# Attention and a gated layer on one core: raw scores of batches 1 to 7 stored with even and odd rows side by side, and the product of W3 and W_out started earlier and by halves of W_out

## The chip, the core and the metric

The kernel runs on one core of a Trainium2 chip. The metric is the device time of one execution in microseconds. Before the change, three runs took 1436.35 to 1438.15 us, with a median of 1437.4 us. The profiled execution took 1441.87 us, and its span from the first to the last instruction is 1439.9 us.

## What is computed

The reference is attention with two head mixings, followed by a layer of four matrices, all in float32. B = 8 batches, H = 12 heads, S = 448 rows and columns of scores, D = 64.

```python
scores = scale * np.matmul(q, k.transpose(0, 1, 3, 2))
scores = np.einsum('bhij,hg->bgij', scores, w_pre)
scores = scores - np.max(scores, axis=-1, keepdims=True)
attn = np.exp(scores)
attn = attn / (np.sum(attn, axis=-1, keepdims=True) + 1e-09)
attn = np.einsum('bhij,hg->bgij', attn, w_post)
x = np.matmul(attn, v)          # then (B, S, H, D) -> (B * S, 768)
...
a = x @ w1
b = x @ w2
h = a * b @ w3
return h @ w_out
```

## The kernel before

**Raw scores.** The product of queries and keys is made per batch b, head pair p and quarter c of the rows (`qk`, L167). One unit (b, p, c) is four matmuls into two PSUM banks, `psq`; ScalarE copies both banks into an SBUF tile `st` (L180, L181), and a store puts `st` into a scratch tensor in device memory, `raw_d[b]`, of the shape (row, head, column). The quarters c = 0, 1, 2 have 128 rows, and c = 3 holds the last 64 rows of two head pairs, so a batch has 18 + 3 = 21 units. `st` has two buffers in each of two pools: one pool serves batches 1 to 7 and the even p of batch 0, the other the odd p of batch 0. Through `raw_d` the scores change their layout, since the mixing of heads needs (row, head) on the partitions.

**Blocks.** The rows of a batch are cut into NB = 45 blocks of IB = 10 rows, the last of 8. Two blocks form one m. `fetch` (L196) loads both blocks of m into a tile `r` (two buffers), as two halves s of five rows by twelve heads, 60 partitions each; `mix` (L215) multiplies by w_pre into the banks `psm`; `largest` (VectorE, L228) and `exp` (ScalarE, L236) follow; `scale` (L240) makes the weights w_post divided by the sums on GpSimd; `post` (L251) multiplies by them into the banks `pso`, and `put` (L273) copies these on ScalarE into `mt` (L275). After every GB = 15 blocks, `av` (L293) multiplies `mt` by V (`psa`, L302).

**The order of the work.** `run` (L744) writes out one program over N = 360 steps n, one per block. An even step n = 2m has `largest` and `exp` of m, an odd one `scale` of m, `post` of m - 1 and `mix` of m + 1. So the distance between the exp of two following m is the length of two steps, and the stages of the trace are cut there: in the profiled execution exp of step 10 starts at 59.31 us, of step 18 at 98.42 us. Within a step the order is: fetch (even steps), stores and loads that are due (`do_later`), one piece of weight conversion, `largest` or `scale`, part of the background matmuls (`advance`), `exp`, the rest of these, `av`, `post`, `mix`, and at last the units `qks[n]`. A unit's store is issued at the start of the next step. All DMAs are issued by SyncE in program order; each waits for the completion of the DMA eight places before it, as they share eight semaphores.

**Which unit in which step.** Batch 0 has c = 0 ahead of the loop, then one unit per step in steps 0 to 14. Batch 1's 21 units start at step 11 with 28/21 steps between two of them (L817), so steps 11 to 13 have two units each. The keys and queries of a pair (`kq`) are loaded six steps ahead of its first unit.

**Fold.** The weights come as float64, read as pairs of int32. `converting` (L133) turns one piece of 384 or 256 columns per step into float32 with four VectorE instructions (L122 to L125) and a square on ScalarE (L111), none in steps with `av`; in the step after, `two_parts` (L128) splits it into a high part (ScalarE, L130) and a low part (GpSimd, L131). From W3 and W_out their product is made, called the fold: 8 columns f of W3 (`fw[f]`, three pieces each) by two halves of W_out (`fo`, eight pieces each), each group (f, half) being 8 x 3 = 24 matmuls of 128x384 (`psf`, L361) into bank 6 or 7, 384 in all. The pieces come in the order: column 0, both halves of W_out, then columns 1 to 7 (L330). `there(p)` (L869) says how many fold matmuls the pieces made so far allow; `share` (L851) spreads the fold over steps FOLD = 18 to 48, as it evens out their TensorE work. The first 24 are made by step 9 as the pieces come.

After step 50 the background is the layer itself (`eg`, `eo`, `e`, L523 to L704); a tail of it follows the last step.

Of the kernel before, what the change touches and what calls it, by code (L numbers as in the profile page):

```python
# [18 lines left out]
IB = 10  # L19
# [31 lines left out]
class Kernel:  # L51
# [115 lines left out]
    def qk(self, b, p, c, banks):  # L167


        nc = self.nc  # L170
        ps = [self.bank(i, f"psq{b}_{p}_{c}_{s}")[:, :S] for s, i in enumerate(banks)]
        for z, (t, q, k) in enumerate(self.parts(b, p, c)):
            for s in range(2):
                rows = slice(s * D, (s + 1) * D)
                nc.tensor.matmul(ps[s][z * PP:(z + 1) * PP], t[rows, q:q + PP], t[rows, k:k + S], start=True, stop=True)  # L175
# [4 lines left out]
        nc.scalar.copy(st[:, 0], ps[0])  # L180
        (nc.vector.tensor_copy if b == c == 0 else nc.scalar.copy)(st[:, 1], ps[1])  # L181
        raw = self.raw_d[b]
        if c == 3:
            def store():
                for z in range(2):
                    nc.sync.dma_start(raw[3 * QT:, 2 * (p + z) - 2:2 * (p + z)], st[z * PP:(z + 1) * PP])
            return store
        n = QT if b or c else FIRST
        return lambda: nc.sync.dma_start(raw[c * QT:c * QT + n, 2 * p:2 * p + 2], st[:n])
# [6 lines left out]
    def fetch(self, m):  # L196
        r = self.rp.tile([128, 2, S], F32, tag="r", name=f"r{m}", bufs=2)
        self.rs[m] = r
        b, t = divmod(2 * m, NB)
        if t + 1 < NB and self.width(2 * m + 1) == IB:  # L200
            src = self.raw_d[b][t * IB:(t + 2) * IB].rearrange("(c s i) h j -> s (i h) c j", c=2, s=2)
            for s in range(2):
                self.nc.sync.dma_start(r[s * PP:s * PP + HK], src[s])
            return
        for c in range(2):
            b, t = divmod(2 * m + c, NB)
            for s in range(2):
                k = self.half(2 * m + c, s)
                src = self.raw_d[b][t * IB + s * IH:t * IB + s * IH + k].rearrange("i h j -> (i h) j")
                self.nc.sync.dma_start(r[s * PP:s * PP + H * k, c], src)  # L210

    def half(self, n, s):
        return min(IH, self.width(n) - s * IH)

# [36 lines left out]
    def post(self, m):  # L251
# [11 lines left out]
        for c in range(2):  # L263
            n = 2 * m + c
            w, (b, t) = self.width(n), divmod(n, NB)
            a, u = divmod(t, GB)
            if u == 0:
                self.mt[b, a] = self.mp.tile([128, NJ, H, GB * IB], F32, tag="mt", name=f"mt{b}_{a}")
            src = self.pso[c][:, :NJ * 2 * HK].rearrange("p (j s g i) -> p j s g i", j=NJ, s=2, g=H)
            dst = self.mt[b, a][:, :, :, u * IB:u * IB + w]  # L270
            self.ends.append((4 + c, lambda dst=dst, src=src, w=w: self.put(dst, src, w)))

    def put(self, dst, src, w):  # L273
        if w == IB:
            self.nc.scalar.copy(dst.rearrange("p j g (s i) -> p j s g i", s=2), src)  # L275
# [54 lines left out]
    def fold_jobs(self):  # L330
# [17 lines left out]

    def folding(self):
        nc = self.nc  # L350
        for f in range(KF):
            for half in range(2):
                w = self.fw[f]

                i = 6 + half
                p = self.bank(i, f"psf{half}_{f}")[:, :DH]
                atoms = [(k, t, x, y) for k in range(KF) for t, (x, y) in enumerate(PAIRS)]
                for k, t, x, y in atoms:
                    if (k, t) != (0, 0):
                        yield  # L360
                    nc.tensor.matmul(p, w[:, k, x], self.fo[:, k, y, half * DH:(half + 1) * DH],  # L361
                                     start=(k == 0 and t == 0), stop=(k == KF - 1 and t == 2))
                z = self.fp.tile([128, 3, 2, 128], F32R, tag="z", name=f"fz{half}_{f}")
                q = p.rearrange("p (d c) -> p d c", c=128)
                dst = self.w34_d[half * 3:(half + 1) * 3, :, f].rearrange("d p t c -> p d (t c)")

                def low(z=z, q=q, dst=dst):
                    nc.vector.tensor_tensor(z[:, :, 1], q, z[:, :, 0].bitcast(F32), op=ALU.subtract)
                    self.later.append(lambda: nc.sync.dma_start(dst, z.rearrange("p d t c -> p d (t c)").bitcast(F32)))

                self.ends.append((i, lambda z=z, q=q: nc.scalar.copy(z[:, :, 0], q)))
                self.soon.append((i, low))
                yield

# [369 lines left out]
    def run(self):  # L744
# [8 lines left out]
        self.ps = self.pool("ps", 1, space=PSUM)  # L753
        self.raw_d = [dp.tile([S, H, S], F32, name=f"raw{b}_d") for b in range(B)]
        self.w_d = [dp.tile([KF, 128, k, 2, 128], F32, name=f"w{i}_d") for i, k in enumerate((K1, K1, KF))]
# [137 lines left out]
        for n in range(N + 6):  # L893
# [48 lines left out]
            elif fold_pieces:  # L942
                f = (self.n_made - 1 - 2 * KF) // 3
                if f < 2 or done >= 2 * KF * 3 * (f - 1):
                    pieces = fold_pieces
# [72 lines left out]
def layouts(inputs):  # L1018
# [37 lines left out]
```

## Time and profile before

| | |
|---|---|
| runs, median (3) | 1437.4 us |
| profiled execution | 1441.87 us, span 1439.9 us |
| TensorE busy | 1386.1 us (96%) |
| VectorE, ScalarE, GpSimd busy | 742.8, 833.3, 622.0 us |
| mean granted TensorE clock | 0.987 |
| DMA | 416.87 MB, queue of SyncE 87.5% of 16 engines' span |

How to read it: a TensorE that is busy nearly all the time bounds the kernel wherever it has no gaps, so the places of interest are the gaps, and what ends them. In a row of the windows view stand the length of the stretch, each engine's busy time with the count of its instructions in brackets, the granted TensorE clock, the mean busy share of the 16 DMA engines and the rate in GB/s. A row of the timeline has start, length, engine, line, operation and operands, and in square brackets the engine's idle time ahead of it with what ended it.

### The profile page before, as it was taken

The numbers are of one execution on the slowest core, as the hardware profiler recorded it, in microseconds if no ns is written. First come the engines' busy times: TensorE is split into PE (matmuls) and PEld (weight loads), VectorE is DVE, ScalarE is ACT, GpSimd is POOL, SyncE is SP. The second block draws the span as 40 slices with busy tenths as digits, with TensorE's granted clock in tenths as the row PEclk, the third lists the DMA queues.
The fourth block names the chain that finished last, engine by engine and source line by source line (L and its number), as shares of the span: only waits on it lengthen the run. The fifth ranks groups of instructions, "written<-read, shape, count | busy, mean of one in ns | idle before, by whom it ended". The sixth has DMA issues, their size and how long they took to land.

```text
span 1439.9 us, 45779 instructions
## 1 busy us (share of the span) xinstructions
PE 1386.1 (96%) x18684; PEld 1056.7 (73%) x18684; DVE 742.8 (52%) x1497; ACT 833.3 (58%) x1952; POOL 622.0 (43%) x754
## 2 busy tenths in 40 slices
PE   5879999999999999999999999999999999999998
PEld 2357786766677767776777777777777777889988
DVE  5957566767644545432344435334444456345563
ACT  4866666767756756665655556556556445432231
POOL 1423233444324544532345345434335436457693
PEclk8989999999999999999999999999999999999999
DMA  8998789999999999999889988799979757698775
GB/s 283 366 319 277 237 266 321 325 312 305 313 280 356 368 357 318 380 348 333 286 266 290 315 289 265 247 316 332 300 229 301 248 174 224 196 327 268 239 234 171
DMA packets 203761, 416.87 MB, mean 290 GB/s; under 512 B 20528, under 2 KB 120112, under 8 KB 203472
## 3 DMA queue, kind: packets, MB, share of 16 engines
q1 hardware_dynamic: 203552, 413.94, 87.5%
q8 instruction: 149, 2.44, 0.7%
q14 instruction: 60, 0.49, 0.1%
HBM read 279.77 MB, written 134.09 MB: 287 GB/s over the span
## 4 chain that ended last, share of the span: by engine, by line
PE 81%; DMA 9%; DVE 5%; ACT 2%; issue 1%; SPq 0%; POOL 0%; DVEq 0%; POOLq 0%; ACTq 0%
PE e L704 20%; PE psa L302 11%; PE pso L261 10%; PE psm L221 8%; PE psq L175 7%; PE eg L523 6%; PE psf L361 4%; PE eo L554 4%; PE e2o L704 4%; PE e3o L704 4%; DMA wu<-w_d 3%; PE e1o L704 3%; DMA raw_d<-st 2%; DMA cs<-wo 2%; DMA r<-raw_d 1%
## 5 line engine op out<-in xcount | busy, mean ns | idle before, releaser
L248 POOL TENSOR_SCALAR w<-wpo,ri 128x60 f32<-128x60 f32 x360 | 180.3, 517 | 482.9 <-DVE ri L246 464.6
L228 DVE TENSOR_REDUCE mn<-psm 128x1 f32<-128x448 f32 x360 | 207.6, 618 | 319.1 <-PE psm L221 318.8
L275 ACT COPY mt<-pso 128x480 f32<-128x480 f32 x352 | 197.8, 621 | 183.6 <-PE pso L261 183.4
L704 PE MATMUL e<-eh,wu 128*128 128x448 f32 x1008 | 297.3, 371 | 4.4 <-DVE c L658 3.2
L236 ACT ACTIVATE e<-psm,mn 128x448 f32<-128x448 f32 x360 | 226.8, 643 | 8.3 <-DVE mn L228 8.3
L704 PEld LDWEIGHTS e<-eh,wu 128*128 128x128 f32 x1008 | 187.5, 188 | 50.9 <-issue 25.1
L221 PE MATMUL psm<-r,wsc 60*64 60x448 f32 (+1 forms) x1440 | 193.1, 552 | 20.7 <-DVE cx L124 7.8
L261 PEld LDWEIGHTS pso<-w,e 60*64 60x64 f32 x10080 | 175.3, 135 | 50.9 <-issue 42.2
L261 PE MATMUL pso<-w,e 60*64 60x60 f32 x10080 | 199.2, 224 | 0.4 <-ACT mt L275 0.3
L704 PE MATMUL e<-el,wu 128*128 128x448 f32 x504 | 186.8, 371 | 0.0
L302 PE MATMUL psa<-mt,v 128*64 128x150 f32 (+1 forms) x2304 | 158.5, 294 | 4.2 <-ACT st L180 4.2
L302 PEld LDWEIGHTS psa<-mt,v 128*64 128x64 f32 x2304 | 145.1, 138 | 20.3 <-ACT st L180 6.9
L175 PE MATMUL psq<-kq 64*64 64x448 f32 x1176 | 156.1, 542 | 4.0 <-ACT st L180 4.0
L658 DVE TENSOR_TENSOR c<-c,e 128x448 f32<-128x448 f32 x168 | 101.6, 617 | 82.5 <-PE e L704 77.9
L180 ACT COPY st<-psq 128x448 f32<-128x448 f32 x162 | 86.5, 534 | 79.7 <-ACT mt L275 34.1
L523 PE MATMUL eg<-xh,wu 128*128 128x448 f32 x384 | 118.8, 380 | 3.3 <-DMA wu<-w_d 3.3
L643 POOL TENSOR_TENSOR el<-x,eh 128x448 fp32r<-128x448 f32 x90 | 104.2, 1174 | 34.4 <-ACT eh L642 28.9
L704 PEld LDWEIGHTS e<-el,wu 128*128 128x128 f32 x504 | 94.6, 188 | 22.2 <-issue 14.1
L175 PEld LDWEIGHTS psq<-kq 64*64 64x64 f32 x1176 | 60.7, 135 | 58.1 <-issue 30.0
L523 PEld LDWEIGHTS eg<-xh,wu 128*128 128x128 f32 x384 | 71.4, 189 | 36.0 <-issue 24.7
L245 DVE TENSOR_SCALAR sa<-sm 128x2 f32<-128x2 f32 x180 | 35.2, 196 | 116.0 <-ACT e L236 115.6
L181 ACT COPY st<-psq 128x448 f32<-128x448 f32 x162 | 87.8, 542 | 0.0
(99 smaller groups left out, 2015.6 us busy)
## 6 DMA issues: line engine op xcount, KB each, us to landing
r<-raw_d SPq DMA_DIRECT2D x344, 210.0 KB, 5.4
raw_d<-st SPq DMA_DIRECT2D x138, 448.0 KB, 6.2
wu<-w_d SPq DMA_DIRECT2D x104, 384.0 KB, 6.4
wu<-s_d SPq DMA_DIRECT2D x96, 384.0 KB, 4.9
wu<-w_d SPq DMA_DIRECT2D x51, 512.0 KB, 6.2
kq<-kq SPq DMA_DIRECT2D x42, 448.0 KB, 7.1
wu<-s_d SPq DMA_DIRECT2D x36, 512.0 KB, 5.0
x<-x_d SPq DMA_DIRECT2D x72, 224.0 KB, 6.4
```

The costliest lines, as they stand in the source:

```text
L175: nc.tensor.matmul(ps[s][z * PP:(z + 1) * PP], t[rows, q:q + PP], t[rows, k:k + S], start=True, stop=True)
L221: nc.tensor.matmul(ps[s][c * PP:(c + 1) * PP, :S], self.wsc[k], r[k, c], start=True, stop=True)
L228: self.nc.vector.tensor_reduce(mn[:, s:s + 1], self.psm[m][s][:, :S], axis=AX.X, op=ALU.min)
L236: nc.scalar.activation(e, p[:, :S], AF.Exp, bias=mn[:, s:s + 1], scale=-1.0, accum_out=sm[:, s:s + 1])
L248: nc.gpsimd.tensor_scalar_mul(w2[:, s], self.wpo, ri[:, s:s + 1])
L261: nc.tensor.matmul(self.pso[c][z * PP:(z + 1) * PP, at:at + HK], e[k, j * PP:(j + 1) * PP], w2s[k, s], start=True, stop=True)
L275: self.nc.scalar.copy(dst.rearrange("p j g (s i) -> p j s g i", s=2), src)
L302: nc.tensor.matmul(self.psa[rows, g % 3, :W], v[:, j, rows], mt[:, j, 2 * g + s, :W], start=(j == 0), stop=(j == NJ - 1))
L523: nc.tensor.matmul(p, u[:, k % (K1 // 2), x], xs[y][:, k], start=(k == 0 and t == 0), stop=(k == K1 - 1 and t == 2))
L643: nc.gpsimd.tensor_tensor(lo, x, hi.bitcast(F32), op=ALU.subtract)
L658: nc.vector.tensor_tensor(a[out], a[to[0]], p, op=ALU.add)
L704: nc.tensor.matmul(p, w[:, k, x], ops[m, k][y], start=(k == 0 and t == 0), stop=(k == nk - 1 and t == 2))
```

## The change

Three things change.

**Raw scores of batches 1 to 7 are interleaved.** `raw_d[b]` has the shape (row pair, head, parity, column) for b > 0. The host orders the query columns so that in each unit the even rows lie on one half of the partitions and the odd ones on the other. A unit's store becomes two DMAs, one per parity (four for c = 3), whose contiguous runs in device memory are one head's 448 columns (1792 bytes) where they were two heads' (3584 bytes). A fetch of two blocks reads ten row pairs: the first block of m gets the even rows and the second the odd ones, and each partition reads one run of 3584 bytes where it read two of 1792. Blocks whose partner lies in another batch or in another group of 15, or is shorter, are fetched singly, with four DMAs. `put` writes `mt` with a stride of two elements for b > 0. Batch 0 stays as it was.

**Fold.** The pieces come as column 0, the first half of W_out, column 1, the second half of W_out, columns 2 to 7. The groups are (0, first half), (1, first half), then columns 0 and 1 with the second half together, k by k, then the others one after another. FOLD is 9.

**Batch 1's units** start at step 15, with 1.15 steps between two of them, so that no step before 48 has more than one unit.

By the rules of the loop, the matmuls of the fold that are done by the end of a step are:

| step | 9 | 11 | 13 | 15 | 17 | 18 | 21 | 24 | 25 | 31 | 41 | 48 |
|---|---|---|---|---|---|---|---|---|---|---|---|---|
| before | 24 | 24 | 24 | 24 | 24 | 43 | 58 | 99 | 106 | 180 | 288 | 384 |
| after | 24 | 42 | 54 | 66 | 78 | 84 | 96 | 114 | 144 | 220 | 305 | 384 |

Of batch 1's units, 6 come by the end of step 17 before, and 3 after.

TensorE, steps 11 and 12, before: the names are psq, batch, pair, quarter, bank. The rows run from the end of step 11 to the end of step 12.

```order
L175 MATMUL psq0_5_2_0_845<-kqz5_134 64x448
L175 MATMUL psq0_5_2_1_846<-kqz5_134 64x448
...
L175 MATMUL psq1_0_0_0_854<-kq1_0_468 64x448
L175 MATMUL psq1_0_0_1_855<-kq1_0_468 64x448
...
L175 MATMUL psq0_1_3_0_887<-kqz0_124 64x448
L175 MATMUL psq0_1_3_1_888<-kqz0_124 64x448
...
L175 MATMUL psq1_0_1_0_896<-kq1_0_468 64x448
L175 MATMUL psq1_0_1_1_897<-kq1_0_468 64x448
```

The same place after; psf is followed by half and column.

```order
L175 MATMUL psq0_5_2_0_863<-kqz5_134 64x448
L175 MATMUL psq0_5_2_1_864<-kqz5_134 64x448
...
L383 MATMUL psf0_1_772<-fo_148,fw1_691 128x384 x6
L175 MATMUL psq0_1_3_0_905<-kqz0_124 64x448
L175 MATMUL psq0_1_3_1_906<-kqz0_124 64x448
...
L383 MATMUL psf1_0_935<-fo_148,fw0_227 128x384 x3
L383 MATMUL psf1_1_936<-fo_148,fw1_691 128x384 x3
```

Two units of batch 1 have gone from between those of batch 0, and twelve fold matmuls of two columns stand between them.

TensorE, steps 22 to 24, before: the folds of steps 22 and 23, the mix of step 23, its unit, and the fold of step 24.

```order
L361 MATMUL psf0_1_1334<-fo_148,fw1_1127 128x384 x14
L361 MATMUL psf1_1_1481<-fo_148,fw1_1127 128x384 x12
...
L221 MATMUL psm12_0_1544<-r12_1309,wsc_138 64x448
L221 MATMUL psm12_1_1545<-r12_1309,wsc_138 64x448
...
L175 MATMUL psq1_2_2_0_1552<-kq1_2_986 64x448
L175 MATMUL psq1_2_2_1_1553<-kq1_2_986 64x448
...
L361 MATMUL psf1_1_1481<-fo_148,fw1_1127 128x384 x12
L361 MATMUL psf0_2_1598<-fo_148,fw2_1451 128x384 x3
```

The same place after, from the fold of step 23 to that of step 25.

```order
L383 MATMUL psf0_2_1519<-fo_148,fw2_1486 128x384 x9
...
L240 MATMUL psm12_0_1557<-r12_1344,wsc_138 64x448
L240 MATMUL psm12_1_1558<-r12_1344,wsc_138 64x448
...
L383 MATMUL psf0_2_1519<-fo_148,fw2_1486 128x384 x9
L175 MATMUL psq1_2_1_0_1607<-kq1_2_1144 64x448
L175 MATMUL psq1_2_1_1_1608<-kq1_2_1144 64x448
...
L383 MATMUL psf0_2_1519<-fo_148,fw2_1486 128x384 x6
L383 MATMUL psf1_2_1646<-fo_148,fw2_1486 128x384 x24
```

In steps 22 and 23 nine fold matmuls are left of 26, since the pieces allow no more, and step 25 has 30 at once.

SyncE, stores of units of batch 1's pair 1, before and after (each row with the number of like DMAs):

```order
L189 DMA raw1_d_63<-st1_1_0_1078 128x896
L104 DMA cs23_1089<-w3t 128x3x256
L189 DMA raw1_d_63<-st1_1_1_1114 128x896
L104 DMA cs24_1118<-w3t 128x2x256
L203 DMA r11_1183<-raw0_d_62 60x2x448 x2
```

```order
L189 DMA raw1_d_63<-st1_1_1_1341 64x2x448 x2
L158 DMA kq1_3_1349<-kq 128x896
L104 DMA cs26_1351<-w3t 128x3x256
L189 DMA raw1_d_63<-st1_1_2_1376 64x2x448 x2
L216 DMA r13_1472<-raw0_d_62 60x2x448 x2
```

A unit's one store has become two of half the size at the same place of the queue.

The diff, cut to its core:

```diff
         raw = self.raw_d[b]
+        if b:
+            n, parts = (PP // 2, ((2 * p - 2, 0), (2 * p, PP))) if c == 3 else (PP, ((2 * p, 0),))
+
+            def store():
+                for h, k in parts:
+                    for z in range(2):
+                        nc.sync.dma_start(raw[c * PP:c * PP + n, h:h + 2, z], st[k + z * n:k + (z + 1) * n])
+            return store
...
+        if self.paired(2 * m):
+            src = self.raw_d[b][t * IH:(t + 2) * IH].rearrange("(s i) h c j -> s (i h) c j", s=2)
+            for s in range(2):
+                self.nc.sync.dma_start(r[s * PP:s * PP + HK], src[s])
+            return
...
+    def paired(self, n):
+
+        t, u = n % NB, (n ^ 1) % NB
+        return n >= NB and n // NB == (n ^ 1) // NB and t // GB == u // GB and self.width(n) == self.width(n ^ 1) == IB
...
+            elif self.paired(n):
+                dst = self.mt[b, a][:, :, :, (u - c) * IB:(u - c + 2) * IB].rearrange("p j g (s i c) -> p c j s g i", s=2, c=2)[:, c]
...
-        yield from columns[0]
         for q in range(2):
+            yield from columns[q]
...
-        for f in range(1, KF):
+        for f in range(2, KF):
...
+        for group in [((0, 0),), ((1, 0),), ((0, 1), (1, 1))] + [((f, half),) for f in range(2, KF) for half in range(2)]:
...
+            for k in range(KF):
+                for f, half in group:
+                    for t, (x, y) in enumerate(PAIRS):
+                        self.nc.tensor.matmul(ps[f, half], self.fw[f][:, k, x], self.fo[:, k, y, half * DH:(half + 1) * DH],
...
-            first, per = (11, 28 / 21) if b == 1 else ((b - 1) * NB - 6, NB / 21)
+            first, per = (15, 1.15) if b == 1 else ((b - 1) * NB - 6, NB / 21)
...
-        FOLD, SWITCH, E_AT = 18, NB + 5, NB + 8
+        FOLD, SWITCH, E_AT = 9, NB + 5, NB + 8
...
-            f, r = divmod(p - 3 - 2 * KF, 3)
-            return 2 * KF * 3 * (1 + f) + (0, 9, 18)[r] if f >= 0 else min(max(3 * (p - 3), 0), KF * 3)
+            f, r = divmod(p - 6 - 2 * KF, 3)
+            if f >= 0:
+                return 2 * KF * 3 * (2 + f) + (0, 9, 18)[r]
+            if p >= 6 + KF:
+                return 2 * KF * 3 + 6 * (p - 6 - KF)
+            return KF * 3 + (0, 9, 18)[p - 3 - KF] if p >= 3 + KF else 3 * max(p - 3, 0)
...
-    kq = np.ascontiguousarray(np.stack([qt.reshape(B, HP, 2 * D, S), kt], axis=3))
+    order = [c + 2 * i + z for c, n in ((0, QT), (QT, QT), (2 * QT, QT), (3 * QT, PP)) for z in range(2) for i in range(n // 2)]
+    kq = np.ascontiguousarray(np.stack([qt.reshape(B, HP, 2 * D, S)[..., order], kt], axis=3))
```

More of the change, by code (lines that the diff above doesn't have):

```diff
@@ L187, in qk @@
             return store
-        n = QT if b or c else FIRST
+        n = QT if c else FIRST
         return lambda: nc.sync.dma_start(raw[c * QT:c * QT + n, 2 * p:2 * p + 2], st[:n])
@@ L199, in fetch @@
         b, t = divmod(2 * m, NB)
-        if t + 1 < NB and self.width(2 * m + 1) == IB:
+        if self.paired(2 * m):
[3 more added lines that the diff above has]
+            return
+        if b == 0 and t + 1 < NB and self.width(2 * m + 1) == IB:
             src = self.raw_d[b][t * IB:(t + 2) * IB].rearrange("(c s i) h j -> s (i h) c j", c=2, s=2)
@@ L208, in fetch @@
                 k = self.half(2 * m + c, s)
-                src = self.raw_d[b][t * IB + s * IH:t * IB + s * IH + k].rearrange("i h j -> (i h) j")
+                raw = self.raw_d[b][t * IH:t * IH + k, :, s] if b else self.raw_d[b][t * IB + s * IH:t * IB + s * IH + k]
+                src = raw.rearrange("i h j -> (i h) j")
                 self.nc.sync.dma_start(r[s * PP:s * PP + H * k, c], src)
     def half(self, n, s):
-        return min(IH, self.width(n) - s * IH)
+        return min(IH, self.width(n) - s * IH) if n < NB else self.width(n) // 2
+    def paired(self, n):
+        t, u = n % NB, (n ^ 1) % NB
+        return n >= NB and n // NB == (n ^ 1) // NB and t // GB == u // GB and self.width(n) == self.width(n ^ 1) == IB
     def mix(self, m):
@@ L269, in post, with put @@
             src = self.pso[c][:, :NJ * 2 * HK].rearrange("p (j s g i) -> p j s g i", j=NJ, s=2, g=H)
[L270 to L274, printed above, removed]
+            if b == 0:
+                dst = self.mt[b, a][:, :, :, u * IB:u * IB + w]
+            elif self.paired(n):
+                dst = self.mt[b, a][:, :, :, (u - c) * IB:(u - c + 2) * IB].rearrange("p j g (s i c) -> p c j s g i", s=2, c=2)[:, c]
+            else:
+                src = src[:, :, :, :, :w // 2]
+                dst = self.mt[b, a][:, :, :, u * IB:u * IB + w].rearrange("p j g (i s) -> p j s g i", s=2)
+            self.ends.append((4 + c, lambda dst=dst, src=src, w=w, b=b: self.put(dst, src, w, b)))
+    def put(self, dst, src, w, b):
+        if b:
+            self.nc.scalar.copy(dst, src)
+        elif w == IB:
             self.nc.scalar.copy(dst.rearrange("p j g (s i) -> p j s g i", s=2), src)
@@ L349, in folding @@
     def folding(self):
-        nc = self.nc
[L351 to L373, printed above, removed]
@@ new lines, in folding @@
+        for group in [((0, 0),), ((1, 0),), ((0, 1), (1, 1))] + [((f, half),) for f in range(2, KF) for half in range(2)]:
+            banks = {g: 6 + (g[0] if g[0] < 2 else g[1]) for g in group}
+            ps = {g: self.bank(banks[g], f"psf{g[1]}_{g[0]}")[:, :DH] for g in group}
+            for k in range(KF):
+                for f, half in group:
+                    for t, (x, y) in enumerate(PAIRS):
+                        self.nc.tensor.matmul(ps[f, half], self.fw[f][:, k, x], self.fo[:, k, y, half * DH:(half + 1) * DH],
+                                              start=(k == 0 and t == 0), stop=(k == KF - 1 and t == 2))
+                        if (k, t) == (KF - 1, 2):
+                            self.fold_out(f, half, banks[f, half], ps[f, half])
+                        yield
@@ new lines, in fold_out, with low @@
+    def fold_out(self, f, half, i, p):
+        nc = self.nc
+        z = self.fp.tile([128, 3, 2, 128], F32R, tag="z", name=f"fz{half}_{f}")
+        q = p.rearrange("p (d c) -> p d c", c=128)
+        dst = self.w34_d[half * 3:(half + 1) * 3, :, f].rearrange("d p t c -> p d (t c)")
+        def low():
+            nc.vector.tensor_tensor(z[:, :, 1], q, z[:, :, 0].bitcast(F32), op=ALU.subtract)
+            self.later.append(lambda: nc.sync.dma_start(dst, z.rearrange("p d t c -> p d (t c)").bitcast(F32)))
+        self.ends.append((i, lambda: nc.scalar.copy(z[:, :, 0], q)))
+        self.soon.append((i, low))
@@ L753, in run @@
         self.ps = self.pool("ps", 1, space=PSUM)
-        self.raw_d = [dp.tile([S, H, S], F32, name=f"raw{b}_d") for b in range(B)]
+        self.raw_d = [dp.tile([S // 2, H, 2, S] if b else [S, H, S], F32, name=f"raw{b}_d") for b in range(B)]
         self.w_d = [dp.tile([KF, 128, k, 2, 128], F32, name=f"w{i}_d") for i, k in enumerate((K1, K1, KF))]
@@ L943, in run @@
                 f = (self.n_made - 1 - 2 * KF) // 3
-                if f < 2 or done >= 2 * KF * 3 * (f - 1):
+                if f < 2 or done >= 2 * KF * 3 * max(f - 1, 2):
                     pieces = fold_pieces
```

## The prediction

> **What bounds the kernel now.** I read the page first: busy time, then the forty slices, each 36 us long.
>
> ```profile
> span 1439.9 us, 45779 instructions
> ...
> PE 1386.1 (96%) x18684; PEld 1056.7 (73%) x18684; DVE 742.8 (52%) x1497; ACT 833.3 (58%) x1952; POOL 622.0 (43%) x754
> ...
> PE   5879999999999999999999999999999999999998
> ...
> PEclk8989999999999999999999999999999999999999
> DMA  8998789999999999999889988799979757698775
> ```
>
> TensorE is idle for 1439.9 - 1386.1 = 53.8 us in all, and its low slices are the first three. So there is little to win after about 110 us, and I cut the beginning into stretches of two steps, from the exp of one m to that of the next.
>
> ```profile
> core 0: us, PE busy (x) PEld busy (x) DVE busy (x) ACT busy (x) POOL busy (x), PEclk, DMA share, GB/s
> ...
> 52.56:59.31 6.75, 4.92 (x91) 2.66 (x90) 6.37 (x13) 6.12 (x16) 3.12 (x5) 1.00 1.02 371
> 59.31:67.45 8.14, 6.74 (x101) 3.44 (x96) 7.69 (x17) 6.77 (x18) 3.20 (x5) 1.00 1.04 379
> 67.45:82.70 15.25, 7.87 (x104) 3.86 (x100) 6.58 (x13) 7.83 (x20) 3.41 (x5) 0.82 1.04 382
> 82.70:88.31 5.61, 4.29 (x80) 2.51 (x76) 5.04 (x10) 5.61 (x16) 3.10 (x5) 0.89 1.03 359
> 88.31:98.42 10.11, 7.83 (x103) 5.75 (x96) 7.68 (x15) 5.84 (x16) 3.14 (x5) 0.96 0.96 323
> 98.42:106.90 8.48, 8.48 (x126) 7.08 (x123) 4.50 (x10) 4.96 (x14) 2.30 (x4) 0.84 0.70 219
> ...
> 116.87:123.97 7.10, 7.10 (x99) 5.79 (x99) 6.64 (x14) 5.20 (x15) 3.12 (x5) 1.00 1.03 322
> ```
>
> Steps 8 and 9 (52.56 to 59.31) go at the pace of VectorE and ScalarE: 6.37 and 6.12 us busy of 6.75. Steps 10 to 17 (59.31 to 98.42) are another matter: no engine is full, TensorE idles 1.40 + 7.38 + 1.32 + 2.28 = 12.4 us, and the DMA engines are at a share of 0.96 to 1.04. From 98.42 us on TensorE is full. What stops steps 12 and 13 stands in the timeline and in the waits from 59 to 98 us.
>
> ```profile
> 71.34 0.53 ACT L180 COPY st<-psq 128x448 f32<-128x448 f32 x1 [2.55 <-DMA raw_d<-st]
> 75.16 0.53 ACT L180 COPY st<-psq 128x448 f32<-128x448 f32 x1 [2.85 <-DMA raw_d<-st]
> 75.74 1.41 PE L175 MATMUL psq<-kq 64*64 64x448 f32 x8 [2.40 <-ACT st L180]
> ```
>
> ```profile
> ACT st L180 <- DMA raw_d<-st: 11.8, 6, 3.6
> PE psq L175 <- ACT st L180: 8.1, 6, 3.3
> ```
>
> ScalarE waits until a store has let go of its buffer st, and TensorE waits for ScalarE with its next unit. The stores are late because the DMA engines are full; from 60 to 98 us the DMA view says:
>
> ```profile
> DMA packets 7128, 13.90 MB, mean 366 GB/s; under 512 B 667, under 2 KB 4251, under 8 KB 7125
> ...
> q1 hardware_dynamic: 7125, 13.85, 101.6%
> ...
> raw_d<-st SPq DMA_DIRECT2D x9, 448.0 KB, 7.2
> ```
>
> So steps 10 to 17 are bound by bytes, and the steps after them by TensorE.
>
> **The change part by part.** *Fold matmuls pulled ahead.* By the table of the loop's rules, 54 fold matmuls (78 - 24) are done by the end of step 17 that were not before, and three units of batch 1 fewer (3 for 6). Their prices:
>
> ```profile
> 130.01 4.71 PE psf L361 x26
> ```
>
> ```profile
> 48.75 0.98 PE L175 MATMUL psq<-kqz 64*64 64x448 f32 x8
> ```
>
> 54 x 4.71 / 26 = 9.8 us leave the part of the program in which TensorE is full, and 3 x 0.98 = 2.9 us enter it: 6.9 us less. What hides them in steps 10 to 17 is the 12.4 us of idle time found above. They fit by time: per two steps there are 12 to 18 of them, 2.2 to 3.3 us, and the two extra units are gone. Each needs its piece split one step earlier by ScalarE and GpSimd, as the early 24 do; these waited little:
>
> ```profile
> L361 PE MATMUL psf<-fo,fw 128*128 128x384 f32 x384 | 76.4, 346 | 2.6 <-POOL fo L131 2.2
> ```
>
> Were the cover gone, the work would only stay as long as it is, elsewhere: between -6.9 and 0 us.
>
> *Bytes.* Three stores of 448 KB leave steps 10 to 17, and one store of a finished fold group (384 KB) enters them; batch 1's loads of keys move three or four steps back on SyncE's queue, with three of them before step 18 as now. Net 960 KB x 1.024 = 0.98 MB, at 366 GB/s 2.7 us. If bytes bind alone, exp of step 18 comes 2.7 us sooner; with the peak of steps 11 to 13 gone up to 4 us (1.4 MB fewer by step 16), if the pace of the conversion or TensorE's new work binds as well, 0. I take -2.0.
>
> *Light steps.* In steps 22 and 23 the pieces allow 9 fold matmuls where 26 stood. These two steps took 7.10 us (from 116.87), all TensorE. Without 17 x 0.181 = 3.1 us they need 4.0, but VectorE and ScalarE need up to 6.75 for two steps (the row from 52.56), so up to 2.7 us are idle. Steps 26, 27, 30 and 31 lose a little more. I take +3.0, between +1 and +5. Steps 25 and 28 with 30 matmuls each cost TensorE nothing extra, only others wait for it there.
>
> *Clock.* From 98.42 to 106.90 TensorE is busy for the whole 8.48 us at a granted clock of 0.84, after stretches half idle. At full clock it would be 8.48 x 0.16 = 1.36 us less. With fewer gaps ahead I take -0.5, between -1.4 and 0. The Trainium skill, "TensorE: Matmul & The Clock Gate", Part 1, says that the array falls to half its clock after an idle window of about 3.4 us and rises again after a busy one. By that the whole 1.36 us would go if no such gap is left, and the sum would be 0.9 us lower; the trace agrees so far that the clock is below 1 only around gaps.
>
> *Interleaving.* From the code, 126 stores become two and 42 become two of half the size again, and 14 more m are fetched with four DMAs: 182 DMAs more. SyncE pays a third of a microsecond for one:
>
> ```profile
> 77.28 0.33 SPq L189 DMA_DIRECT2D raw_d<-st  x1
> ```
>
> 60 us over the span, on a queue that waits for TensorE most of the time. Loads have half as many runs, stores twice as many, with nearly equal bytes; if a run costs a fixed time, the two cancel. Where bytes are dense this could show, since the DMA engines are nearly full from 400 to 800 us:
>
> ```profile
> 400.00:600.00 200.00, 196.71 (x3048) 146.46 (x3048) 98.53 (x204) 129.40 (x307) 91.66 (x106) 0.98 0.99 342
> 600.00:800.00 200.00, 196.93 (x2872) 147.03 (x2865) 76.19 (x173) 120.49 (x286) 73.70 (x102) 0.99 0.94 309
> ```
>
> But there TensorE idles only 3.3 + 3.1 us. The trace has no such store; half of the idle time, -3, is the bound for a gain, and 1% of these 400 us, +4, for a loss. I take 0. The copies into mt with a stride of two elements are bounded by ScalarE's nearest rows, the square that reads every second word and the cast of as many neighbouring ones:
>
> ```profile
> L111 ACT ACTIVATE cm<-cs 128x384 f32<-128x384 f32 x64 | 36.3, 568 | 15.1 <-DVE cx L125 8.7 <-DMA cs<-wo 6.3
> L130 ACT CAST fw<-cx 128x384 fp32r<-128x384 f32 x16 | 8.4, 525 | 5.2 <-DVE cx L125 5.2
> ```
>
> 43 ns for 384 words is 0.05 us for 480, beside a TensorE that is full: nothing.
>
> *Sum:* -6.9 - 2.0 + 3.0 - 0.5 + 0 = -6.4 us. The profiled execution of 1441.87 us would take 1435.5; it lies 4.5 us above the runs' median, so the median goes from 1437.4 to 1431.0. The ends of the terms that count give about 1427 to 1435 for this case.
>
> **The rivals.** *A, more is won:* bytes give the whole 4 us, the light steps cost only 1, the clock gives 1.4, and the longer reads bring nothing. -6.9 - 4 + 1 - 1.4 = -11.3, 1426.1 us. For it speaks that the worst stretch, 15.25 us, holds the doubled units that go; against it that the DMA engines were never idle in it.
>
> *B, the idle time comes back:* the conversion's pace and the fold's waits for its pieces keep steps 10 to 17 at 39 us, and the light steps idle for 5. -6.9 + 5 = -1.9, 1435.5 us. That is also what is left if the early fold does not do what the order says, and only stands in TensorE's queue waiting for GpSimd. For it speaks that two steps never took less than 5.61 us; against it the 2.2 us of waits for GpSimd in the whole fold.
>
> *C, slower: the halved stores hold st longer.* Batch 1's units now come nearly every step from 15 to 38, on two buffers. If the second half of a store lands only after the first, a buffer is held for two landings:
>
> ```profile
> raw_d<-st SPq DMA_DIRECT2D x138, 448.0 KB, 6.2
> ...
> raw_d<-st SPq DMA_DIRECT2D x48, 224.0 KB, 4.9
> ```
>
> 9.8 us, where one takes 6.2. With 1.1 us of copies that is 10.9 us against two steps of 8.5 (from 98.42): ScalarE waits 2.4 us per two units, 24 us for 21 units, and TensorE 8.1 / 11.8 of that, as in the waits above: 16.5 us. -6.4 + 16.5 = +10.1, 1447.5 us. It decides once ScalarE's waits for st are above 9.3 us more than now. The Trainium skill, "DMA: Bandwidth & Descriptors", Rules for kernel authors, says of two transfers to disjoint halves of the partitions not to bother, as they serialize on the same engines, and to use one of 128 partitions; by it C would be the outcome if each half also paid its fixed cost anew. No run here shows a store split so; the nearest rows, of c = 3, are of two DMAs of 64 partitions that land within 4.9 us, issued together, and that speaks for an overlap and against C.
>
> **How the numbers follow.** My forecast has a chance of 0.58, A 0.12, B 0.18, C 0.10, and 0.02 is for what I don't see. The likeliest gives 1431.0 us. The range runs from 1425 (A, and the bounds of bytes and interleaving together) to 1439 (B with a loss by the interleaving); C lies outside. A measurement of this kernel can tell about 0.2%, 2.9 us, from no change. Faster than 1434.5: nearly all of the forecast, A, and a little of B, 0.70. Within 2.9 us: most of B and the edge of the forecast, 0.19. Slower: C and the worst of the interleaving, 0.11.
>
> **What would show it.** Right: exp of step 18 at 94 to 98 us, with no wait for st above 3 us between steps 10 and 17 and the fold's matmuls lying in what were gaps; a gap of TensorE of 2 to 3 us in steps 22 and 23; the clock near 1 at step 18; and the distance from there to the end shorter by about 4 us, with stages after 260 us as long as they were within 3 us. Wrong: exp of step 18 later than 99 us (B), waits for st from step 15 to 38 above 9 us more than now (C), or the stages from 400 to 800 us longer or shorter by more than 4 us, which would be the interleaving.

## The result, and the profile after

The changed kernel took 1455.92 us (median of 4 runs, 1454.51 to 1457.18) beside 1437.78 us of the kernel before on the same chip; the ratio is 1.013 [1.0114, 1.0146]. The change made the kernel slower by 18 us, where 1431 us had been forecast, and 1439 was the end of the range. All ratios here and below leave out six single executions of 1902 to 6806 us, far above the others of the same kernel. The profiled execution took 1454.51 us, 12.6 us more than that of before. The page, busy time and slices:

```profile
span 1452.6 us, 46031 instructions
...
PE 1389.6 (96%) x18684; PEld 1053.1 (72%) x18684; DVE 744.3 (51%) x1497; ACT 847.5 (58%) x1945; POOL 623.9 (43%) x754
...
PE   5889998999999989999999999999999999999999
```

TensorE is idle for 1452.6 - 1389.6 = 63.0 us, 9.2 more than before, and busy for 3.5 us more with the same 18684 matmuls. The first slices are fuller than before, and no later slice looks bad: the loss is spread over places too short for this view. The first steps of after, cut from exp to exp of steps 8, 10, 12 and so on up to 24:

```profile
58.40:65.70 7.30, 7.30 (x105) 4.42 (x103) 6.85 (x17) 5.97 (x15) 3.06 (x5) 1.00 1.04 374
65.70:77.70 12.00, 7.15 (x97) 4.01 (x92) 7.47 (x14) 6.47 (x17) 3.22 (x5) 0.90 1.04 385
77.70:85.70 8.00, 8.00 (x99) 4.92 (x92) 6.32 (x12) 5.94 (x15) 3.09 (x5) 0.73 1.02 371
85.70:92.20 6.50, 6.25 (x100) 3.68 (x92) 6.15 (x12) 5.97 (x15) 3.48 (x5) 1.00 0.86 254
92.20:101.80 9.60, 8.80 (x142) 5.81 (x134) 5.13 (x11) 5.61 (x15) 1.97 (x4) 1.00 0.92 298
101.80:111.50 9.70, 7.83 (x131) 5.73 (x128) 5.71 (x12) 6.38 (x17) 2.07 (x4) 1.00 0.80 230
111.50:119.60 8.10, 7.42 (x90) 5.42 (x88) 5.33 (x13) 4.88 (x13) 3.48 (x5) 0.79 0.92 274
```

Steps 10 to 17 now take 33.8 us (58.4 to 92.2) in place of 39.1, so exp of step 18 comes at 92.2 us, sooner than forecast. TensorE's idle time there fell from 12.4 to 5.1 us. But steps 18 to 23, where it was nearly full before, now hold 0.80 + 1.87 + 0.68 = 3.35 us of idle time, and the granted clock is 0.79 in the last two. The dense stages lose too; a window of after:

```profile
400.00:600.00 200.00, 190.90 (x2935) 140.73 (x2935) 97.25 (x200) 128.97 (x298) 90.81 (x104) 0.99 0.99 330
```

From 400 to 600 us TensorE is busy for 190.90 us where it was for 196.71. What it waits for, and what ScalarE waits for, stands in the waits of after (for each pair, the total in us, how many times, and the longest):

```profile
PE psm L240 <- DMA r<-raw_d: 8.8, 7, 3.1
PE eg L550 <- DMA wu<-w_d: 8.3, 5, 3.4
ACT st L180 <- DMA raw_d<-st: 12.9, 8, 4.6
```

and in those of before:

```profile
PE psm L221 <- DMA r<-raw_d: 5.5, 4, 2.4
PE eg L523 <- DMA wu<-w_d: 3.3, 3, 2.0
ACT st L180 <- DMA raw_d<-st: 16.2, 10, 3.6
```

The waits for fetched scores and for weights grew by 8.3 us together, nearly all of the 9.2. The waits of ScalarE for a store, on which rival C rested, became shorter. So the sign was C's, and the mechanism was not.

### The profile page after: what moved, and what is told of

Its sections match the earlier page's. It is cut to its first block, busy times and chain, and to the rows that moved or that the text cites. A ratio compares the mean times of both kernels' runs of the same rounds, so it can differ in the third digit from the quotient of the medians.

```text
span 1452.6 us, 46031 instructions
## 1 busy us (share of the span) xinstructions
PE 1389.6 (96%) x18684; PEld 1053.1 (72%) x18684; DVE 744.3 (51%) x1497; ACT 847.5 (58%) x1945; POOL 623.9 (43%) x754
## 2 busy tenths in 40 slices
DMA packets 208352, 416.90 MB, mean 287 GB/s; under 512 B 23461, under 2 KB 126357, under 8 KB 208061
## 4 chain that ended last, share of the span: by engine, by line
PE 75%; DMA 14%; DVE 4%; ACT 3%; issue 1%; SPq 1%; POOL 1%; DVEq 0%; ACTq 0%; POOLq 0%
PE e L731 18%; PE psa L329 10%; PE pso L280 9%; PE psm L240 8%; PE psq L175 7%; PE eg L550 5%; DMA r<-raw_d 4%; PE e2o L731 4%; PE e1o L731 4%; PE psf L383 4%; PE e3o L731 4%; PE eo L581 3%; DMA wu<-w_d 2%; ACT e L255 1%; DMA x<-x_d 1%
## 5 line engine op out<-in xcount | busy, mean ns | idle before, releaser
L300 ACT COPY mt<-pso 128x480 f32<-128x480 f32 x315 | 190.7, 672 | 177.6 <-PE pso L280 177.3
L180 ACT COPY st<-psq 128x448 f32<-128x448 f32 x162 | 86.7, 535 | 70.2 <-PE psq L175 29.4
L383 PEld LDWEIGHTS psf<-fo,fw 128*128 128x128 f32 x384 | 66.8, 192 | 42.0 <-issue 9.7
L383 PE MATMUL psf<-fo,fw 128*128 128x384 f32 x384 | 83.6, 358 | 9.4 <-POOL fo L131 3.3
```

The lines of the kernel that those rows point to most:

```text
L300: self.nc.scalar.copy(dst, src)
L383: self.nc.tensor.matmul(ps[f, half], self.fw[f][:, k, x], self.fo[:, k, y, half * DH:(half + 1) * DH], start=(k == 0 and t == 0), stop=(k ...
```

## The experiments

Theory: the interleaving costs the time, since it puts more and dearer transfers into SyncE's queue (T1), or since the runs of its stores are shorter (T2), or by its further parts, the fetches with four transfers and the strided copies (T3). Rival: the early part moves later work into collisions. Ratios are to the kernel before on the same chip, and 1% is 14.4 us. The numbers that later expectations quote of earlier runs go partly by medians, and can differ from the ratios by 1 us.

**e1, the fold and the units alone** (the old layout of the scores, with `fold_jobs`, `folding`, `there`, FOLD = 9 and the later units of after).

> Only the fold's new order and the new schedule of batch 1's units, with the old layout of the scores. The trace of after is 2.8 us ahead at step 50, where the fold ends, and loses from step 136 on, in single stalls of TensorE. Theory (the interleaving is what costs): about 3 us faster than before, 1435 us (1432 to 1437), with stages after 260 us as long as before. Rival (the early part shifts later work into collisions, the interleaving is innocent): slower than before, 1445 to 1456 us.

Measured: 1.0005 [0.999, 1.002]. The early part is innocent of the 18 us, but it wins nothing either, where some 3 us were expected.

**e2, the interleaving alone** (`raw_d`, stores, fetch, copies and host order of after; the fold and units of before).

> Only the interleaved layout of batches 1 to 7, with the old fold and the old units. Theory (interleaving): 15 to 21 us slower than before, 1453 to 1459 us, with the stalls of TensorE for r and wu from 480 us on. Rival (the two parts only cost together, by more transfers at the same moment): under 8 us slower, 1438 to 1446 us.

Measured: 1.0123 [1.0098, 1.0148], 17.7 us. With e1 that is the whole loss, and the two parts add up.

**e3, halved stores in the old layout.**

```
+        if b:
+            def store():
+                for z in range(2):
+                    nc.sync.dma_start(raw[c * QT + z * PP:c * QT + (z + 1) * PP, 2 * p:2 * p + 2], st[z * PP:(z + 1) * PP])
+            return store
```

> The kernel before, with each store of 128 partitions of batches 1 to 7 cut into two of 64, as the change does, but with the old layout: bytes, runs of 3584 bytes and fetches are as before. Theory T1 (SyncE's queue: a unit's store costs it 1.16 us where it cost 0.34, and fetches and weight loads are issued later): 10 to 20 us slower, 1448 to 1458 us. Theory T2 (the DMA engines: shorter runs in the stores): within 3 us of before. Theory T3 (strided copies, more fetches of four transfers): within 3 us.

Measured: 1.0051 [1.003, 1.0071], 7.3 us: less than T1 expected, more than the others. The store alone, with bytes and runs as before, costs.

**e4, short runs alone** (heads stored as `(s p)`; the host puts w_pre and batch 0's heads in that order).

```
+        raw = raw.rearrange("i (s p) j -> i s p j", s=2)
+        return lambda: nc.sync.dma_start(raw[c * QT:(c + 1) * QT, :, p], st)
```

> The kernel before, with the heads of the scores in DRAM put in another order, so that a store of a unit is one transfer of 128 partitions as before but of two runs of 1792 bytes each, where it had one of 3584; the number of transfers and the fetches are as before. T1 (SyncE's queue counts transfers): within 4 us of before, unless SyncE's price goes by runs; then its store rows show it. T2 (the DMA engines pay by the run): 10 to 25 us slower, 1448 to 1463 us (more than in after, whose fetches got longer runs in return). T3: within 3 us.

Measured: 1.0023 [1.0006, 1.0041], 3.3 us, the side of T1. T2 alone is out.

**e5, the fetches and the copies alone.**

```
-        if t + 1 < NB and self.width(2 * m + 1) == IB:
+        if t + 1 < NB and self.width(2 * m + 1) == IB and (b == 0 or self.paired(2 * m)):
...
+        if b and w == IB:
+            self.nc.scalar.copy(dst.rearrange("p j g (i s) -> p j s g i", s=2), src)
```

> The kernel before, with the other two parts of the interleaving: the fetches of those 14 m that the change no longer pairs take four transfers in place of two, and the copies into mt have a stride of two elements (the columns within a block of ten then stand in another order, so the output is permuted). Stores as before. Theory T3 (these two carry what split stores, 0.51%, and short runs, 0.23%, leave open of the 1.23%): 5 to 8 us slower than before. Rival T1 x T2 (the stores' price grows when both come together): within 3 us of before.

Measured: 0.9994 [0.9976, 1.0012]. T3 is out. The copies did get longer, as forecast (mean 672 ns in after for 621 in before), beside a TensorE that is full.

**e6, the stores of after with the old fetches and copies** (e4, each store cut by partitions: 64 + 64, at c = 3 32 + 32).

> The stores exactly as after has them in number and run length (each of the 126 in two of 64 partitions, the 42 in two of 32, all in runs of 1792 bytes), with the old fetches in runs of 1792 bytes and the old copies. T1 x T2 (the stores alone cost it all, and the longer runs of the fetches bring nothing): 15 to 20 us slower than before. T3: 9 to 12 us slower, the sum of the two parts measured apart. If the longer runs of the fetches do bring something, it is above 20 us.

Measured: 1.015 [1.0126, 1.0174], 21.5 us. The stores alone cost it all, more than e3 and e4 together. Against e2 the longer runs of the fetches may give some 4 us back, but the two intervals overlap.

**e7 and e8, the second of each pair of stores from another queue,** in the changed kernel.

```
-                        nc.sync.dma_start(raw[c * PP:c * PP + n, h:h + 2, z], st[k + z * n:k + (z + 1) * n])
+                        (nc.scalar if z else nc.sync).dma_start(raw[c * PP:c * PP + n, h:h + 2, z], st[k + z * n:k + (z + 1) * n])
```

> The changed kernel, with the second of each pair of stores issued from ScalarE's queue, not from SyncE's: transfers, bytes and runs are those of after. T1 (SyncE's queue is what delays fetches and weight loads): at least half of the 18 us come back, 1437 to 1447 us, and SyncE waits longer for free buffers r again (towards the 283 us of before, from 188). T2 (the DMA engines): 1452 to 1459 us as after. A third way: ScalarE pays 0.6 us for each of 168 transfers and waits for free places, and hands the loss on through exp: 1450 to 1470 us with ScalarE's own waits grown.

> The same with the second stores issued from GpSimd. T1: at least half of the 18 us come back, 1437 to 1447 us. T2: 1452 to 1459 us. Third way: GpSimd's issue is dearer than SyncE's and delays the scaled weights of post and the low parts of weights, 1450 to 1475 us.

Measured: with ScalarE 1.0384 [1.0358, 1.0409], with GpSimd 1.0063 [1.0039, 1.0087]. From GpSimd half of the loss comes back, the lower end of what T1 expected. It is no clean proof, since this queue also packs its transfers otherwise (196929 DMA packets where after has 208352). From ScalarE the third way came true, and at 1492.93 us dearer than the 1450 to 1470 expected; its issues in e7:

```profile
L189 ACTq DMA_DIRECT2D raw_d<-st x168: 309/602/988, 85.8 to 1141.2; - x168
```

168 x 0.6 = 101 us on an engine whose exp and copies TensorE waits for.

**e9, a small extra transfer behind each store** (e4, with 15 KB per store into DRAM that nobody reads).

```
             def store():
                 nc.sync.dma_start(raw[c * QT:(c + 1) * QT, :, p], st)
+                nc.sync.dma_start(self.extra_d[b, p, c], self.wpo[:PP])
```

> e4 (one store of 128 partitions in runs of 1792 bytes) with a small extra transfer of 15 KB behind each store of batches 1 to 7, into DRAM that nobody reads: as many transfers as e6, but none of its halves. Theory P (what costs is a further transfer in SyncE's queue: its issue of about 0.58 us, and one of the eight places, since each transfer waits for the one eight before it): 12 to 24 us slower than before. Rival S (halved transfers of short runs are slow on the DMA engines themselves): within 3 us of e4, so 2 to 7 us slower than before.

Measured: 1.0172 [1.0153, 1.0191], 24.7 us. Transfers that carry next to nothing cost as much as the halves.

**e10, stores cut by head** (`st[:, y]`, all 128 partitions, for y in 0, 1).

> The kernel before, with each store of batches 1 to 7 cut in two by head, not by partition: two transfers of 128 partitions (64 at c = 3), one run of 1792 bytes in each; number of transfers and runs as in e6. If the cut into halves of the partitions is what makes e6 dear: at most the sum of e3 and e4, 5 to 12 us slower than before. If number and run length decide, whatever the cut: 16 to 26 us, as e6.

Measured: 1.01 [1.0087, 1.0114], 14.4 us, between the two expectations: a cut into halves of the partitions isn't needed for the cost, and e6 is dearer still.

**e11, the fold with its bursts capped,** in e1.

```
-                now = max(min(there(p), KF * 3 + wanted) - done, 0)
+                now = min(max(min(there(p), KF * 3 + wanted) - done, 0), 19 - n % 2 * 10)
```

> e1 (the old layout, the fold pulled ahead, the later units) with at most 19 fold matmuls in an even step and 9 in an odd one, so the bursts of 30 in steps 25 and 28 go. If the bursts delay what others wait for, 2 to 4 us faster than e1, so 1432 to 1434 us. If what was won by step 18 is lost to fold matmuls that come in small groups and wait for their pieces, as the trace of e1 has it (9.2 us of idle time before them where the old order has 2.9), no change to e1 within 2 us.

Measured: 1.0000 [0.9988, 1.0012]. The bursts were not the cause.

**e12, all stores whole, from GpSimd.**

> The kernel before, with the 168 stores of batches 1 to 7 issued from GpSimd, whole as they were. SyncE then has fewer transfers than before and its eight places are free for fetches and weights. If SyncE's queue already costs time before the change, in steps 140, 148 and 194, where equal work took up to 5 us longer in one execution than in another: 3 to 8 us faster than before. If GpSimd's 0.66 us for each, and its waits for st, delay the weights of post: slower by 2 to 10 us.

Measured: 1.0041 [1.0023, 1.0058], slower. SyncE's relief is there (it waits 347.7 us for free buffers r), but GpSimd pays for each:

```profile
L189 POOL DMA_DIRECT2D raw_d<-st x126: 539/606/762, 65.8 to 1084.1; - x126
```

Which of GpSimd's work is late by this stays open.

**e13 and e14, the number of transfers in long runs:** e13 is the kernel before with e9's extra transfers, e14 is e3 with the stores of c = 3 halved as well.

> The kernel before, its stores whole and in runs of 3584 bytes, with a small extra transfer of 15 KB behind each store of batches 1 to 7: the number of transfers alone (1460, as e6 and e9). If the number alone decides: 16 to 24 us slower than before, as e9 (23.6). If run length counts with it (e3, of 1418 transfers in long runs, lost only 7.4): 5 to 12 us slower.

> e3 with the stores of c = 3 halved too (1460 transfers, all runs 3584 bytes). If the 42 further transfers make the difference between e3 (7.4) and e6 (21.6): 15 to 22 us slower than before. If run length does: 6 to 11 us.

Measured: e13 1.0116 [1.0096, 1.0136], 16.7 us; e14 1.0113 [1.0092, 1.0133], 16.2 us. Both fall where the number of transfers decides: 168 more of them cost some 16 us, whether they carry half a store or nothing that is needed, and that is nearly all of e2's 17.7.

**e15 and e16, other transfers taken out of the queue,** in the kernel before: loads of keys and values (90), or stores of split weights (64), from GpSimd.

```
-        self.nc.sync.dma_start(t, self.v[b, g])
+        self.nc.gpsimd.dma_start(t, self.v[b, g])
```

> The kernel before, with the loads of keys and values (90 transfers, which never waited for an engine in SyncE's queue) issued from GpSimd. If fewer transfers in SyncE's queue are worth on this side what more of them cost on the other (0.06 to 0.14 us each): 3 to 8 us faster than before. If GpSimd's issue of 0.66 us each delays the weights of post: slower by up to 4 us.

> The kernel before, with the stores of split weights (w_d and the s_d of 384 KB, 64 transfers), whose data GpSimd itself wrote last, issued from GpSimd. They lie in the dense stages before 700 us, and SyncE waited 28.9 us for them: 3 to 8 us faster than before if SyncE's order holds fetches back there, no change within 2 us if those waits were off the path.

Measured: e15 0.9984 [0.9967, 1.0001]; e16 1.0036 [1.002, 1.0051]. Below the number that the kernel has, 90 fewer transfers bring some 2.3 us (the interval reaches from 4.7 us faster to no change). In e16 neither expectation came true: it is 5.2 us slower, so what GpSimd pays outweighs any gain, and whether the 28.9 us that SyncE waited there lay on the path stays open.

**e17 and e18, loads of keys and values from GpSimd,** in the changed kernel, and in e11.

> The changed kernel, with the loads of keys and values (90 transfers) issued from GpSimd as in e15; its stores stay halved and in short runs. If the number of transfers in SyncE's queue decides (182 more in after): about half of the 18 us come back, 1443 to 1449 us. If the place matters more than the number (these loads are issued far ahead, and the stores stand where fetches and weights wait): less than 5 us come back, 1450 to 1455 us.

> A version that should be at least as fast as both kernels: the old layout of the scores, the fold pulled ahead with its bursts capped (e11), and the loads of keys and values issued from GpSimd (e15). Sum of the two measured parts: -0.1 and -2.6 us, so 1433 to 1436 us, 0 to 4 us faster than before. If the early part has more use for the freed queue, where transfers fill it: 5 us faster or more.

Measured: e17 1.0097 [1.0077, 1.0117], so some 5 us of the 18.7 come back, and the place counts beside the number. e18 0.9985 [0.9969, 1.0002], 1432.93 us (1429.35 to 1438.94) beside 1435.93: the fastest version, clearly ahead of after, but not to be told from before.

## Where the time goes

SyncE's own rows show what changed in its queue (SPq). A unit's store cost the queue 0.34 us in before, and costs two issues of 0.58 in after:

```profile
L189 SPq DMA_DIRECT2D raw_d<-st x138: 319/343/1640, 29.5 to 1077.8; - x138
```

```profile
L189 SPq DMA_DIRECT2D raw_d<-st x336: 302/581/1697, 85.0 to 1096.1; - x168
```

(The columns are count, shortest, median and longest in ns.) How much room the queue has is told by its waits from 130 to 1300 us: the time in which a fetch stood ready and waited only for TensorE to free r. The rows of before, fetches with two transfers and with four:

```profile
SPq L203 <- PE psm L221: 283.0, 102, 6.5
SPq L210 <- PE psm L221: 5.3, 2, 3.4
```

and those of after, where the fetches of batch 0 (L216) have a line of their own:

```profile
SPq L211 <- PE psm L240: 187.6, 79, 6.0
SPq L224 <- PE psm L240: 8.1, 3, 3.7
SPq L216 <- PE psm L240: 5.3, 3, 3.4
```

104 such waits in before are 85 in after, and their 288.3 us are 201.0; in e13 they are 220.4 us, in e15 317.8. The other fetches were held up by something else, such as what stood ahead of them in the queue. Most of this costs nothing, and the room alone does not order the losses: e3 has 214.2 us and lost 7.3, e13 has more room and lost 16.7. The cost falls on few places. Against the mean of before, e1 and e5, the trace of after takes 18.1 us longer from exp 52 to exp 358; of the 153 stretches of two steps between them 128 differ by at most 0.2 us, and eight (from steps 58, 136, 146, 168, 178, 192, 282 and 284) hold 14.9 us. In that from step 192, for one, TensorE waits for r for 3.1 us in after and 4.2 in e13, 2.4 in before and not at all in e5. How such a stall comes about, steps 136 to 140 show in e5 and e6. SyncE's timeline in e5 (stores whole, as in before), up to the exp of step 138 at 492.1 us:

```profile
484.46 0.32 SPq L189 DMA_DIRECT2D raw_d<-st  x1
485.08 1.09 SPq L400 DMA_DIRECT2D wu<-w_d  x2
...
487.65 1.59 SPq L203 DMA_DIRECT2D r<-raw_d  x2
489.95 0.34 SPq L189 DMA_DIRECT2D raw_d<-st  x1
490.82 0.34 SPq L400 DMA_DIRECT2D wu<-w_d  x1
```

and in e6 (stores halved), where that exp is at 497.2 us:

```profile
490.18 1.63 SPq L194 DMA_DIRECT2D raw_d<-st  x2
491.90 1.68 SPq L407 DMA_DIRECT2D wu<-w_d  x2
...
494.63 1.51 SPq L216 DMA_DIRECT2D r<-raw_d  x2
496.23 1.39 SPq L194 DMA_DIRECT2D raw_d<-st  x2
499.33 0.35 SPq L407 DMA_DIRECT2D wu<-w_d  x1
```

TensorE next needs the first of the two weight loads. It is issued 4.7 us before TensorE runs out of work in e5 (at 489.73) and 2.9 us before in e6 (at 494.78). The two halves ahead of it occupy the queue for 1.63 us, where the whole store takes 0.32; that is up to 1.3 of these 1.8 us, and not surely all of it, since the views of e6 name a wait of 0.9 us for VectorE beside these two loads. The load also takes longer to land; its row in the chain view (releasers followed back) of e5 and of e6 has the start and the time to landing:

```profile
485.08 6.60 DMA wu<-w_d
```

```profile
491.90 7.37 DMA wu<-w_d
```

TensorE stands until it has landed, 2.00 us in e5 and 4.53 us in e6; one row of each timeline:

```profile
491.73 0.47 PE L529 MATMUL eg<-xh,wu 128*128 128x448 f32 x1 [2.00 <-DMA wu<-w_d]
```

```profile
499.31 0.74 PE L536 MATMUL eg<-xh,wu 128*128 128x448 f32 x1 [4.53 <-DMA wu<-w_d]
```

So 1.8 us of later issue and 0.8 us of longer landing make the 2.5 us by which the gap grew. The order of eight shows in the load behind it. In the program each transfer of this queue waits for the one eight places before it. The load issued at 499.33 in e6 stands eight places behind that of 491.90 and starts when that one has landed, at 499.27; the row of SyncE's waits names it:

```profile
SPq L407 <- DMA wu<-w_d: 1.7, 1, 1.7
```

TensorE has no further gap in these steps, so here the late place cost nothing.

The first columns of the windows behind these gaps (granted clock third from the end), e5 and then e6:

```profile
491.70:495.20 3.50, 3.47 (x12) 2.90 (x12) 1.26 (x4) 2.65 (x8) 2.09 (x3) 0.69 1.04 381
495.20:498.70 3.50, 3.50 (x45) 3.19 (x46) 0.00 (x0) 0.00 (x0) 2.35 (x3) 0.83 1.05 374
```

```profile
499.30:502.80 3.50, 3.49 (x9) 3.15 (x10) 1.70 (x2) 0.11 (x1) 3.29 (x4) 0.50 1.01 331
502.80:506.30 3.50, 3.50 (x40) 2.97 (x40) 0.00 (x0) 0.00 (x0) 0.00 (x0) 0.85 1.01 323
```

The clock takes (0.31 + 0.17) x 3.5 = 1.7 us in e5 and (0.50 + 0.15) x 3.5 = 2.3 in e6. The gap's 2.5 us and the clock's 0.6 make the 3.0 us by which steps 138 and 139 are longer in e6 (13.9 for 10.9). A stall costs more than its length. Single executions scatter here: the same two steps took 8.4 us in before and 9.9 in after. The Trainium skill, "TensorE: Matmul & The Clock Gate", Part 1, has the clock halved after an idle window of about 3.4 us; behind the gap of 4.53 us the trace agrees (0.50), and behind the one of 2.00 us it shows a shorter dip as well.

Whether it is the issue time or the places that holds the queue up, two rows weigh, and they don't decide. Stores of e10 (by head) and of e14 (halves, long runs), both with 168 more transfers:

```profile
L196 SPq DMA_DIRECT2D raw_d<-st x252: 319/376/1659, 71.6 to 1084.5; - x126
```

```profile
L194 SPq DMA_DIRECT2D raw_d<-st x252: 445/556/1589, 72.5 to 1085.9; - x126
```

An issue of 0.38 us costs nearly as much in time (14.4 us) as one of 0.56 (16.2). That speaks for the number of transfers, each of which takes a place in the order of eight until it has landed. It doesn't rule the issue's price out: e10 has short runs as well, which alone cost 3.3 us in e4, and in the stall above the halves' issues stood ahead of the late load. A transfer of 15 KB keeps its place as long as one of 210; the issues of e13, with the median time to landing at the end:

```profile
r<-raw_d SPq DMA_DIRECT2D x344, 210.0 KB, 5.3
...
extra_d<-wpo SPq DMA_DIRECT2D x168, 15.0 KB, 5.1
```

So it is shown that the stores halved in SyncE's queue cost the time, and that further transfers with hardly any bytes cost as much; by which of the two ways stays open. A run with more than eight places could have told; it wasn't tried. Open is also why the last 42 transfers (e3 to e14) cost 9 us where the first 126 cost 7, and how much short runs add, by themselves or by a dearer issue (3.3 us in e4, 8.0 from e13 to e9, 5.3 from e14 to e6, nothing from e14 to e10).

## Why the prediction was wrong, step by step

*Interleaving, taken as 0, between -3 and +4:* here it failed. The prediction had the 182 transfers, priced them at 60 us of a queue "that waits for TensorE most of the time", and let that cover hide them. Measured are 17.7 us (e2). The cover was misread: in before the rows of SyncE's waits for TensorE add up to 455 us of the 1440, and from 400 to 600 us to 32 of 200. It was also a sum over the span, while the cost falls on few places. And the price was that of one issue for 128 partitions (0.33 us), while one for a half takes 0.58, and each takes a place until it lands. The bound for a loss, 1% of 400 us, had no row behind it. (The count of 182 is right, but the new fetches with four transfers are 7 m, not 14: the loads of r went from 376 to 390.)

*Fold pulled ahead, -6.9:* too large. With the bytes, the light steps and the clock it was to win 6.4 us; e1, which has these parts alone, was 0.7 us slower, within its interval of no change. The price of 0.181 us came from 26 matmuls in a row. In e1 they run in groups of a few; two rows of its timeline, between 79 and 93 us:

```profile
79.47 2.29 PE L356 MATMUL psf<-fo,fw 128*128 128x384 f32 x6
...
91.57 1.32 PE L356 MATMUL psf<-fo,fw 128*128 128x384 f32 x6
```

0.22 to 0.38 us each, the dearer row in steps 14 and 15, where the clock was 0.69 in e1. The group as a whole, in e1 and then in e5 (the old order), up to 230 us:

```profile
L356 PE MATMUL psf<-fo,fw 128*128 128x384 f32 x384 | 83.2, 357 | 9.2 <-POOL fo L131 3.3 <-DVE fz L369 2.2 <-POOL fw L131 1.7
```

```profile
L367 PE MATMUL psf<-fo,fw 128*128 128x384 f32 x384 | 77.0, 348 | 2.9 <-POOL fo L131 2.4
```

6.2 us more busy time and 6.3 us more idle time before it, some of it for its pieces (POOL, fo and fw). Rival B is nearest to what came of this part: its "fold's waits for its pieces" and its light steps are there, but not its steps 10 to 17 at 39 us, which took 34.8 in e1. How much each of these waits cost wasn't tested apart.

*Bytes, -2.0, and the date of exp 18:* right in direction, too small. It came at 92.2 us (93.4 in e1), where the six executions of before and e2 to e6, with the old order, had it at 95.4 to 98.4. One wait for st of 4.6 us was left in steps 10 to 17, where none above 3 us was expected.

*Light steps, +3.0:* right in kind, too small. From exp 18 to exp 24 e1 took 27.4 us and e5 23.8, though the traces have 21 fold matmuls fewer there in e1 (30 for 51) and one unit more, 21 x 0.181 - 0.98 = 2.8 us less work: some 6.4 us lost, among them 3.4 us of idle time and, at a clock of 0.79 in the last two steps, 1.7 us.

*Clock, -0.5:* the dip wasn't saved but moved, to 0.73 in steps 14 and 15 and 0.79 in steps 22 and 23.

*Rival C:* it drew its loss from waits for st, which fell (16.2 to 12.9 us). The halves land beside each other, within 5.1 us each in e3 (median), where a whole store took 6.2 in before. The Trainium skill, "DMA: Bandwidth & Descriptors", Rules for kernel authors, was right that one transfer of 128 partitions is better than two halves, but what the runs show as the reason is not that they serialize: extra transfers of 15 KB cost the same.

*The comparison itself:* at step 52 after looks 2.7 us ahead of the trace of before (229.6 and 232.3 us), but the six executions with the old order (before, e2 to e6) have that exp at 227.7 to 232.3. What looked like a gain is the spread of single executions.

## What to carry to other kernels

Count what a change adds to the one queue that also carries the just-in-time loads, and look for cover in the densest steps, not in the sum over the span: here 168 transfers of 15 KB, with no work behind them, cost 1.2%. Price a matmul that is moved into gaps by the smallest group in which it will run, with its waits for operands, not by a long burst. A transfer split in two is not free because its bytes are the same.

## What the runs showed of the hardware that was not expected

A transfer of 15 KB took 5.1 us (median) from issue to landing, nearly as long as one of 210 KB with 5.3 (e13). What an issue costs SyncE differed with its form: 0.34 us (median) for 128 partitions with one run each (before), 0.52 with two runs (e4), 0.58 for 64 partitions with one run (e3). The form is not all, since the same 15 KB transfer cost 0.45 us in e13 and 0.61 in e9. An issue of a store cost GpSimd 0.61 us (e12) and ScalarE 0.60 (e7). Behind a gap of 2.0 us the granted clock of TensorE already fell, to 0.69 over the next 3.5 us (e5), and behind one of 4.5 us to 0.50 (e6).
